# One line of scheduling: hand-written instruction order or the Tile scheduler's, in a fused linear-attention and SoLU kernel

## The chip, the cores and the metric

The kernel runs on one core of one Trainium2 chip. The metric is the device time of one execution in microseconds. Before the change the median of 3 runs is 242.95 us (242.89 to 244.39).

## The reference, cut to what matters

```
kv  = einsum('bhsd,bhse->bhde', k, v)           # per batch and head, 64 x 64
o   = einsum('bhsd,bhde->bhse', q, kv)
x   = o / sqrt(mean(o*o, -1) + 1e-6) * g_norm   # norm over the 64 columns of a head
x   = x.transpose(0,2,1,3).reshape(4608, 512)   # 8 batches x 576 tokens, 8 heads x 64
h   = x @ w_in                                  # 512 -> 1024
sm  = exp(h - max) / (sum(exp(h - max)) + 1e-9)
s   = h * sm
ln  = (s - mean(s)) / sqrt(var(s) + 1e-6) * g_ln
out = ln @ w_out                                # 1024 -> 512
```

All inputs and the output are float32. q, k and v are 8 x 8 x 576 x 64.

## The kernel before

The 4608 tokens are worked in nine chunks of 512. Chunk c below 8 holds the first 512 tokens of batch c; chunk 8 holds the last 64 tokens of all eight batches, which the code calls the remainders (`krem`, `vrem`, `qrem`). Tokens lie along the free dimension, features along the partitions.

One chunk passes these steps. `kv_mm` (L143) multiplies keys and values of a batch, and `kv_evac` (L164) copies the result into a block-diagonal tile `kvbd`. `qT` (L172) transposes the queries on TensorE in two halves and VectorE copies each half out. `o_mm` (L191) multiplies the two, one of four head pairs at a time, and ScalarE squares the result (`osq`). `s_mm` (L206) averages the squares over a head by a matmul; ScalarE takes logarithm and exponential (`lss`, `rst`), and VectorE scales into `x_sb`. `h_step` (L220) makes one of eight 128-feature blocks of h with four matmuls; ScalarE takes the exponential `e_sb`, VectorE multiplies to `u_sb`, and GpSimd (POOL) squares it (`usq_sb`, L236) and adds two exponentials (`es_sb`, L238). `stats` (L242) sums squares, values and exponentials over the features with 20 matmuls that each fill one of four 32-column strips of the array; `stats_t` (L257) turns the sums over and makes the per-token factor `rstd`. `out_half` (L279) is the second large product, eight matmuls for 128 tokens in two halves; `out_evac` (L289) scales by `rstd` and stores. The centring of `w_out` (`w_out_mean` L303, `w_out_center` L308) is done once.

There are 51 loads, all issued by POOL, whose instruction stream also holds the squares and sums: eight each of `qs`, `ks` and `vs` (L74, 512 tokens of a batch), eight each of `qrem`, `krem` and `vrem` (L82), two for `w_in` (L97) and one for `w_out` (L138). `ks`, `vs` and `qs` have three buffers each; the remainders have tiles of their own, with no buffer to wait for. The output is stored from SyncE. In PSUM, the tag `st` has one buffer, shared by `kv_ps`, `qT_ps`, `sum_ps` and `st_ps`; h has two, the output two, and `o_ps` with `s_ps` three.

The order is written out by hand. `at(c, s, fn, ...)` (L317) enters a step into a plan under chunk c and slot s; the loop at L384 calls `h_step(c, s)` and then what the plan holds for that slot. So each chunk's h steps are interleaved with the second product of the chunk before and with keys, transposes and norms of the chunks after it. The first 13 loads are written before the loop; the loads of batches 2 to 7 stand in the plan (L354 to L361). The line `tc.manual_schedule()` (L48) makes each engine keep its instructions in the order in which this code issues them.

Where that line is missing, the Tile scheduler orders every engine's instructions when the program is built. It walks along an estimated timeline and gives each engine that is free the earliest-written instruction whose inputs and buffers are ready in that estimate. The order that comes out is fixed in the program. Waits on data and buffers stay, so each engine still works its list from the front.

Of the kernel before, what the change touches and what calls it, by code (L numbers as in the profile page):

```python
# [18 lines left out]
def kernel(  # L19
# [25 lines left out]
    NC = B + 1  # L45
    REM = S - 512

    ctx.enter_context(tc.manual_schedule())  # L48
    big = ctx.enter_context(tc.tile_pool(name="big", bufs=1))
    kvl = ctx.enter_context(tc.tile_pool(name="kvl", bufs=3))  # L50
    ql = ctx.enter_context(tc.tile_pool(name="ql", bufs=3))
# [368 lines left out]
```

## Time and profile before

| | us |
|---|---|
| median of 3 runs | 242.95 |
| the profiled execution | 243.18 |
| its span, first to last instruction | 241.3 |
| TensorE (PE) busy | 199.5 (83%) |
| POOL busy | 159.4 (66%) |
| VectorE (DVE) busy | 138.0 (57%) |
| ScalarE (ACT) busy | 121.5 (50%) |

Busy times of different engines overlap. Matmuls are pipelined, so their busy times overlap among themselves too; four matmuls of 512 columns that run back to back end 0.86 us apart from the next four. 1.88 us of the profiled execution lie outside its span.

### The profile page before, as it was taken

To read this page: it belongs to the slowest core of one execution; us is meant where nothing else is said; L and a number is where in the kernel's file an instruction comes from. 1 tells how busy PE (TensorE), PEld (TensorE's weight loads), DVE (VectorE), ACT (ScalarE), POOL (GpSimd) and SP (SyncE) were. 2 spreads that over 40 slices of the span, in tenths; PEclk is the share of its full clock that TensorE was granted. 3 is DMA by queue.
4 is the path that set the end of the run, shared out by engine and by line. 5 is a ranking of instruction groups with operands and counts; after the bars stand their busy time and mean duration, and the time that the engine had idled before them with its cause. 6 is when DMAs were issued, how large, how long until landed. Compare 5 with 4: busy or idle time off the path is not lost.

```text
span 241.3 us, 3920 instructions
## 1 busy us (share of the span) xinstructions
PE 199.5 (83%) x1536; PEld 95.1 (39%) x1536; DVE 138.0 (57%) x254; ACT 121.5 (50%) x199; POOL 159.4 (66%) x165
## 2 busy tenths in 40 slices
PE   0164899557989997998999899899979989979971
PEld 0141244223444453444445444444535444444420
DVE  0723462593458756674775667487466755755431
ACT  2019453740377646666476666657667577343000
POOL 8640299574766697879959987375756738758500
PEclk9998599965999999999999999999999999999979
DMA  6999969599995289629945992021111202202233
GB/s 66 175 198 196 292 190 182 77 173 144 148 104 110 87 100 175 121 87 151 190 96 93 174 171 90 1 87 46 45 43 46 87 0 90 87 0 87 90 87 88
DMA packets 45682, 27.00 MB, mean 112 GB/s; under 512 B 14944, under 2 KB 40544, under 8 KB 45664
## 3 DMA queue, kind: packets, MB, share of 16 engines
q0 software_dynamic: 39216, 17.30, 55.9%
q1 hardware_dynamic: 6448, 9.44, 11.9%
q8 instruction: 12, 0.20, 0.4%
q14 instruction: 6, 0.05, 0.1%
HBM read 32.51 MB, written 9.44 MB: 174 GB/s over the span
## 4 chain that ended last, share of the span: by engine, by line
PE 53%; ACT 19%; DVE 16%; issue 6%; POOL 4%; POOLq 0%; ACTq 0%
PE out_ps L284 18%; PE h_ps L227 18%; ACT rst L212 5%; ACT lss L210 5%; ACT e_sb L234 5%; PE sum_ps L249 4%; DVE x_sb L213 4%; PE qT_ps L182 4%; PE mean_ps L306 3%; DVE kvbd L168 2%; ACT osq L204 2%; DVE u_sb L235 2%; PE s_ps L208 2%; PE o_ps L197 2%; DVE ob L292 1%
## 5 line engine op out<-in xcount | busy, mean ns | idle before, releaser
L236 POOL TENSOR_TENSOR usq_sb<-u_sb 128x512 bf16<-128x512 bf16 x72 | 75.0, 1043 | 62.4 <-DVE u_sb L235 62.1
L234 ACT ACTIVATE e_sb<-h_ps,zero_t 128x512 f32<-128x512 f32 x72 | 49.1, 682 | 69.8 <-PE h_ps L227 67.4
L227 PE MATMUL h_ps<-x_sb,w_in_sb 128*128 128x512 bf16 x288 | 78.1, 393 | 4.7 <-DVE x_sb L213 4.7
L284 PE MATMUL out_ps<-w_out_sb,u_sb 128*128 128x512 bf16 x288 | 75.9, 391 | 3.7 <-DVE ob L292 3.7
L235 DVE TENSOR_TENSOR u_sb<-h_ps,e_sb 128x512 bf16<-128x512 f32 x72 | 49.4, 686 | 46.4 <-ACT e_sb L234 46.3
L238 POOL TENSOR_TENSOR es_sb<-e_sb 128x512 bf16<-128x512 f32 x36 | 45.7, 1270 | 0.0
L227 PEld LDWEIGHTS <-w_in_sb 128*128 128x128 bf16 x288 | 27.9, 102 | 42.8 <-issue 15.4
L284 PEld LDWEIGHTS <-u_sb 128*128 128x128 bf16 x288 | 27.1, 100 | 38.9 <-issue 11.9
L213 DVE SCALAR_TENSOR_TENSOR x_sb<-o_ps,g_rep,rst 128x512 bf16<-128x512 f32 x36 | 27.0, 751 | 24.9 <-ACT rst L212 24.9
L204 ACT ACTIVATE osq<-o_ps,zero_t 128x512 bf16<-128x512 f32 x36 | 24.1, 678 | 15.6 <-PE o_ps L197 15.5
L292 DVE TENSOR_SCALAR ob<-out_ps,rstd 128x512 f32<-128x512 f32 x36 | 26.7, 743 | 4.8 <-PE out_ps L284 4.0
L212 ACT ACTIVATE rst<-lss,zero_t 128x512 f32<-128x512 f32 x36 | 26.0, 722 | 1.2
L210 ACT ACTIVATE lss<-s_ps,eps_t 128x512 f32<-128x512 f32 x36 | 24.5, 681 | 0.5 <-PE s_ps L208 0.5
L182 PE MATMUL qT_ps<-ident,qs 128*64 128x128 bf16 x256 | 11.5, 238 | 15.5 <-POOL ident masks.py:199 7.6
L208 PE MATMUL s_ps<-osq,head_mean 128*128 128x512 bf16 x36 | 13.7, 392 | 10.7 <-ACT osq L204 9.7
L182 PEld LDWEIGHTS <-qs 128*64 128x64 bf16 x256 | 9.1, 120 | 21.4 <-issue 13.9
L187 DVE COPY qT_sb<-qT_ps 128x1024 bf16<-128x1024 bf16 x18 | 12.3, 681 | 2.4 <-PE qT_ps L182 2.4
L197 PE MATMUL o_ps<-qT_sb,kvbd 128*128 128x512 bf16 x32 | 12.5, 411 | 1.0 <-DVE kvbd L168 1.0
L273 ACT ACTIVATE lv<-vare,zero_t 128x4 f32<-128x4 f32 x9 | 2.7, 297 | 20.6 <-DVE vare L269 20.6
L254 DVE COPY sums<-sum_ps 128x512 f32<-128x512 f32 x9 | 6.2, 691 | 8.4 <-PE sum_ps L249 8.4
L261 PEld LDWEIGHTS st_ps<-stat_pick,sums 128*128 128x128 f32 x72 | 9.3, 191 | 2.2 <-DVE qT_sb L187 0.9
L150 PEld LDWEIGHTS <-ks 128*64 128x64 bf16 x256 | 5.5, 123 | 9.7 <-issue 7.6
(49 smaller groups left out, 131.5 us busy)
## 6 DMA issues: line engine op xcount, KB each, us to landing
out_dram<-ob SPq DMA_DIRECT2D x32, 256.0 KB, 2.4
qs<-in_q_dram POOLq DMA_DIRECT2D x8, 512.0 KB, 6.4
ks<-in_k_dram POOLq DMA_DIRECT2D x8, 512.0 KB, 6.1
vs<-in_v_dram POOLq DMA_DIRECT2D x8, 512.0 KB, 8.5
w_out_f<-in_moe_w_out_dram POOLq DMA_DIRECT2D x1, 2048.0 KB, 19.4
w_in_sb<-in_moe_w_in_dram POOLq DMA_DIRECT2D x2, 512.0 KB, 12.3
out_dram<-ob SPq DMA_DIRECT2D x8, 128.0 KB, 2.3
krem<-in_k_dram POOLq DMA_DIRECT2D x8, 64.0 KB, 5.4
```

Of the source, the lines that this page charges most:

```text
L182: nc.tensor.transpose(t[hh * 64:hh * 64 + 64, pp, cols], qs[c][:, 2 * p + hh, j, :], ident[:, :])
L204: nc.scalar.activation(out=osq[:, :], in_=t[:, :], func=AF.Square, bias=zero_t[:, :])
L210: nc.scalar.activation(out=lss[:, :], in_=t[:, :], func=AF.Ln, bias=eps_t[:, :])
L212: nc.scalar.activation(out=rst[:, :], in_=lss[:, :], func=AF.Exp, scale=-0.5, bias=zero_t[:, :])
L213: nc.vector.scalar_tensor_tensor(out=x_sb[c][:, p, :], in0=o_ps.pop((c, p))[:, :], scalar=g_rep[:, :], in1=rst[:, :], op0=MUL, op1=MUL)
L227: nc.tensor.matmul(t[:, :], w_in_sb[:, dt, f * 128:(f + 1) * 128], x_sb[c][:, dt, :], start=(dt == 0), stop=(dt == NP - 1),)
L234: nc.scalar.activation(out=e[:, f % 2, :], in_=t[:, :], func=AF.Exp, bias=zero_t[:, :])
L235: nc.vector.tensor_tensor(out=u_sb[c][:, f, :], in0=t[:, :], in1=e[:, f % 2, :], op=MUL)
L236: nc.gpsimd.tensor_tensor(out=usq_sb[c][:, f, :], in0=u_sb[c][:, f, :], in1=u_sb[c][:, f, :], op=MUL)
L238: nc.gpsimd.tensor_tensor(out=es_sb[c][:, f // 2, :], in0=e[:, 0, :], in1=e[:, 1, :], op=ADD)
L284: nc.tensor.matmul(t[:, :], u_sb[c][:, f, m * 128:(m + 1) * 128], w_out_sb[:, f, :], start=(f == 0), stop=(f == NF - 1),)
L292: nc.vector.tensor_scalar_mul(out=ob[:, :], in0=t[:, :], scalar1=rstd_sb[c][:, m:m + 1])
```

## The change

The line that asks for the hand-written order is taken out. Nothing else is edited: the same instructions are issued by the same code, in the same written order, with the same tiles and buffers.

```diff
     NC = B + 1
     REM = S - 512
 
-    ctx.enter_context(tc.manual_schedule())
     big = ctx.enter_context(tc.tile_pool(name="big", bufs=1))
     kvl = ctx.enter_context(tc.tile_pool(name="kvl", bufs=3))
```

## Rows read from the trace of the kernel before

**Rows 1.** The page, busy time: us, share of the span, instructions.

```profile
PE 199.5 (83%) x1536; PEld 95.1 (39%) x1536; DVE 138.0 (57%) x254; ACT 121.5 (50%) x199; POOL 159.4 (66%) x165
```

**Rows 2.** Windows: us, busy of PE, PEld, DVE, ACT, POOL, granted clock, DMA share, GB/s.

```profile
40.00:60.00 20.00, 13.26 (x88) 5.85 (x87) 10.76 (x17) 7.11 (x11) 12.63 (x14) 0.75 1.17 135
100.00:120.00 20.00, 18.99 (x158) 9.23 (x155) 14.05 (x25) 12.65 (x22) 17.26 (x19) 1.00 0.86 124
```

**Rows 3.** Timeline of the start: start us, us, engine, line, instruction, [idle before <- releaser].

```profile
7.58 1.13 DVE L123 CAST stat_pick<-ident 32x3 f32<-32x3 bf16 x4 [5.92 <-POOL ident masks.py:199]
...
13.77 0.68 POOL L82 DMA_DIRECT2D vrem<-in_v_dram  x1 [1.77 <-DMA vs<-in_v_dram]
14.22 1.07 PE L150 MATMUL kv_ps<-vs,ks 128*64 128x64 bf16 x32 [0.78 <-DVE qT_sb L187]
...
15.31 0.91 POOL L138 DMA_DIRECT2D w_out_f<-in_moe_w_out_dram  x1
...
27.94 1.04 POOL L236 TENSOR_TENSOR usq_sb<-u_sb 128x512 bf16<-128x512 bf16 x1 [11.71 <-DVE u_sb L235]
```

**Rows 4.** DMA issues at 3.19, 7.49, 8.39 and 13.77 us: size, us to landing.

```profile
vs<-in_v_dram POOLq DMA_DIRECT2D x1, 512.0 KB, 10.3
...
ks<-in_k_dram POOLq DMA_DIRECT2D x1, 512.0 KB, 14.6
...
vs<-in_v_dram POOLq DMA_DIRECT2D x1, 512.0 KB, 16.4
...
vrem<-in_v_dram POOLq DMA_DIRECT2D x1, 64.0 KB, 11.9
```

**Rows 5.** The page, DMA issues: the load of `w_out`.

```profile
w_out_f<-in_moe_w_out_dram POOLq DMA_DIRECT2D x1, 2048.0 KB, 19.4
```

**Rows 6.** The page, costliest groups: busy us, mean ns | idle before, releaser.

```profile
L236 POOL TENSOR_TENSOR usq_sb<-u_sb 128x512 bf16<-128x512 bf16 x72 | 75.0, 1043 | 62.4 <-DVE u_sb L235 62.1
...
L238 POOL TENSOR_TENSOR es_sb<-e_sb 128x512 bf16<-128x512 f32 x36 | 45.7, 1270 | 0.0
```

**Rows 7.** Load issues by line: ns min/median/max on POOL, first and last start us.

```profile
L74 POOL DMA_DIRECT2D ks<-in_k_dram x8: 892/942/943, 2.3 to 128.5; - x8
...
L82 POOL DMA_DIRECT2D qrem<-in_q_dram x8: 722/726/729, 71.8 to 139.9; - x8
```

**Rows 8.** Timeline of PE, 42 to 64 us.

```profile
46.49 0.38 PE L208 MATMUL s_ps<-osq,head_mean 128*128 128x512 bf16 x1 [1.39 <-ACT osq L204]
...
48.98 0.38 PE L208 MATMUL s_ps<-osq,head_mean 128*128 128x512 bf16 x1 [1.89 <-ACT osq L204]
...
50.59 0.59 PE L227 MATMUL h_ps<-x_sb,w_in_sb 128*128 128x512 bf16 x1 [0.81 <-DVE x_sb L213]
...
55.76 1.06 PE L182 MATMUL qT_ps<-ident,qs 128*64 128x128 bf16 x16 [2.16 <-DVE kvbd L168]
56.75 1.89 PE L284 MATMUL out_ps<-w_out_sb,u_sb 128*128 128x512 bf16 x4
58.43 1.91 PE L227 MATMUL h_ps<-x_sb,w_in_sb 128*128 128x512 bf16 x4
...
61.24 0.62 PE L249 MATMUL sum_ps<-usq_sb,stat_sel 128*32 128x512 bf16 x8
...
62.44 1.04 PE L227 MATMUL h_ps<-x_sb,w_in_sb 128*128 128x512 bf16 x4
```

**Rows 9.** The chain of waits, one chunk: start us, us, what.

```profile
106.00 0.86 PE out_ps L284 x4
106.86 1.19 PE sum_ps L249 x20
...
128.07 1.19 PE sum_ps L249 x20
```

**Rows 10.** Timeline, the one longer PE wait inside that chunk.

```profile
114.47 0.38 PE L208 MATMUL s_ps<-osq,head_mean 128*128 128x512 bf16 x1 [0.75 <-ACT osq L204]
```

## The prediction

> **What bounds the kernel now.** I read the busy shares first, then stretches of 20 us, then the chain of waits, then the timelines of the stretches that stood out. PE is the busiest engine with 199.5 us of 241.3, POOL the second with 159.4 [rows 1]. From about 85 us on PE is full: 18.99 us of 20 at a granted clock of 1.00 [rows 2]. There one chunk takes 128.07 - 106.86 = 21.2 us, and the chain runs from one PE group to the next at 0.86 us per four matmuls [rows 9]; the only longer wait that PE has inside that chunk is 0.75 us for a square [rows 10]. So a new order can win little there and can only lose by giving PE something that isn't ready. What is loose is the front. Up to 28 us the kernel waits for its first loads and for one chain of dependent steps. Between 40 and 60 us PE is busy for 13.26 us and its granted clock averages 0.75 of full speed [rows 2]: it waits 1.39, 1.89, 0.81 and 2.16 us for ScalarE and VectorE steps of chunk 1 [rows 8], 6.25 us in all. A greedy order attacks just these waits, and it also moves POOL's loads.
>
> **The start, -0.7 us.** VectorE's casts at 7.58 us waited 5.92 us for the identity matrix [rows 3], and everything written behind them stood still, the clearing of `kvbd` included, which needs no input. A scheduler that takes what is ready does that clearing first, and the copies of the transposed queries come earlier. The product of keys and values started at 14.22 us after 0.78 us of waiting for such a copy [rows 3]. Its own input, the first `vs`, was issued at 3.19 us and landed 10.3 us later [rows 4], at 13.49. So the gain stops there: 14.22 - 13.49 = 0.7 us. Bounds 0 and -0.7; I take all of it.
>
> **POOL's loads and the first squares, +5.1 us.** This is the step that I think decides. POOL issues 51 loads from the same stream as the squares. In the hand order 13 are issued by 16.2 us (the last at 15.31 for 0.91) and the first square follows at 27.94, after 11.71 us in which POOL had nothing to do [rows 3]. The scheduler will not leave that hole. 23 loads need no buffer to come free: `ks`, `vs` and `qs` of batch 2 (third buffers), the 12 `krem` and `vrem` of batches 2 to 7, and the 8 `qrem`. They are ready from the start and go ahead of the first square. On POOL they take 3 x 0.94 + 20 x 0.73 = 17.4 us [rows 7]. But an issue also waits: the eleventh load stood 1.77 us, up to 13.77 us, for the third to land [rows 3], 0.3 us after that landing. So a load waits for the one eight before it. The landings go in order: the second `ks` at 7.49 + 14.6 = 22.1 us, its `vs` at 8.39 + 16.4 = 24.8, the second `vrem` at 13.77 + 11.9 = 25.7 [rows 4], `w_out` at 15.31 + 19.4 = 34.7 [rows 3, 5]. That is 2.7 us for a load of 512 KB and 0.45 us for each of the two remainders after it. After 34.7 the 23 take 3 x 2.7 + 20 x 0.45 = 17.1 us, up to 51.8. The last of the 23, number 36, waits for number 28, which lands 8 x 0.45 earlier at 48.2. With its own 0.73 us the first square starts at 48.9 instead of 27.94.
>
> Who waits: the sums of chunk 0 need its 8 squares and 4 additions, 8 x 1.043 + 4 x 1.270 = 13.4 us of POOL [rows 6]. They would be done at 62.3. The hand order reached these sums at 61.24 us [rows 8], so this alone costs 62.3 - 61.2 = 1.1 us. If `ks`, `vs` and `qs` of batch 3 go ahead too (their buffers are free once batch 0 has been used, near 15 us), 3 x 2.7 = 8.1 us more pass: 70.4, and the cost is 9.2 us. Whether they go ahead hangs on when the estimate has the first square ready, which no row shows. The bounds are +1.1 and +9.2 (and 0, if POOL's order stays as it was); nothing is nearer to either, so I take the middle, 5.1. PE's queue is what stands behind: the sums share the one `st` buffer with the transposes of chunk 2, and behind them stand chunk 1's h steps and chunk 0's output.
>
> By the Trainium skill's page "DMA: Bandwidth & Descriptors", section "Anatomy of one DMA — SWDGE (gpsimd) path", a load takes some 2.0 us plus its bytes over 436 GB/s, an estimate of 6.8 us for `w_out`; loads would then land early and this term would be near zero. The trace has 19.4 us for that load [rows 5], behind others in the queue, and the measurement decides.
>
> **The clock, +1.7 us.** After the waits of 46 to 56 us the next groups of four took 1.89 and 1.91 us, where 62.44 has 1.04 [rows 8]: half speed, the lower of PE's two levels (1.2 against 2.4 GHz), 0.85 + 0.87 = 1.7 us. A PE that waits for POOL at the sums pays the like once more. Bounds 0 and 1.7; the wait is longer than those in the rows, so I take 1.7.
>
> **The gaps at 46 to 56 us, 0.** The scheduler can pull transposes, `o_mm` and `s_mm` of chunk 1 into PE's idle time before 40 us. Worth up to 6.25 us [rows 8], but whatever PE wins before the sums of chunk 0 it then waits for POOL. That cover is the delay above; without it the 6.25 us are won. Bounds 0 and -6.25.
>
> **Steady chunks and the end, 0.** From the second chunk on PE has a backlog, and the earliest written of what is ready is the hand order again. Bounds per chunk: -0.75, the wait above [rows 10], and +3.1 (a rival below). SyncE's stores keep their order. The end is a chain through POOL's last squares in either order.
>
> **The sum.** -0.7 + 5.1 + 1.7 = +6.1 us on the profiled execution's 241.3 us span, 247.4; with the 1.88 us outside the span 249.3. That execution took 243.18, 0.23 above the median, so against the median 242.95 + 6.1 = 249.0.
>
> **Rivals.** *The gaps close and POOL is not late: faster.* If the scheduler's estimate has POOL as busy with loads as the chip shows, the first square stays near 28 us and chunk 1 is ready when chunk 0 ends: -0.7 - 6.25 = -7, 236.0 us. For it speaks that these waits are long and that the work to fill them exists; against it that the filling matmuls hang on loads that land at 25 us and later [rows 4], and a PE that has them in front stands still. The point that decides is the number of loads ahead of the first square. With 33, the last waits for number 25 at 46.9 us, the squares are done near 61 and nothing is lost; with 25, it waits for number 17 at 41.0, they are done at 55.1 and all of the 6.25 us is won.
>
> *Nothing measurable: about 242.4 us.* The written order is already the order of readiness, only the -0.7 us remains.
>
> *The strips are pulled apart: much slower.* The 20 sums take 1.19 us because four strips run at a time; one by one, at 0.86 / 4 = 0.215 us each, they would take 4.3, so 3.1 us more per chunk [rows 9]. A scheduler that places each sum when its square is done scatters them between other matmuls. If half of the gain is lost, 1.55 x 9 = 14 us: 257. The Trainium skill's page "TensorE: Matmul & The Clock Gate", Part 3, states that matmuls on different column groups run concurrently when issued together; 20 in 1.19 us agrees. Against this rival: with a backlog on PE the squares are all there when the sums' turn comes.
>
> **The numbers.** Forecast case 0.38 (by itself 244 to 253 us), faster rival 0.30 (230 to 240), no change 0.17, strips 0.15 (250 to 270). The predicted time is the forecast's, 249.0 us. The range of 8 in 10 leaves out the lower third of the faster rival and some two thirds of the strips' case: 234 to 259. About 1% (2.4 us) is what runs of this kernel tell from no change: faster 0.30, within it 0.17, slower 0.53.
>
> **What would show it.** POOL's first square near 49 to 57 us with more than 33 loads before it; a PE wait for POOL at the first sums; a clock below full behind it. Wrong, if the first square stays near 28 us, if PE has no wait for POOL, or if the steady chunk moves from 21.2 us by more than 0.8: then the change lives where I put zero.

## The result, and the profile after

The changed kernel is **faster**: 233.93 us (median of 4 runs, 233.62 to 235.9) against 242.99 (median of 4, 242.89 to 244.39) of the kernel before on the same chip, a ratio of 0.9636 with a 95% interval of 0.9581 to 0.9691. The prediction was 249.0 us, range 234 to 259, so it missed the sign. The profiled execution took 233.9 us with a span of 231.9, 9.4 us less than the span of before.

Line numbers after are one less than before. The page's busy times:

```profile
PE 197.1 (85%) x1510; PEld 95.6 (41%) x1536; DVE 142.3 (61%) x254; ACT 120.9 (52%) x199; POOL 159.6 (69%) x165
```

Two windows, with the columns of [rows 2]:

```profile
40.00:60.00 20.00, 18.36 (x115) 8.07 (x117) 15.10 (x24) 12.25 (x20) 19.32 (x20) 1.00 0.94 111
100.00:120.00 20.00, 19.77 (x170) 9.70 (x172) 14.37 (x26) 13.07 (x22) 15.78 (x15) 1.00 0.72 129
```

PE has the same work in a shorter span. Between 40 and 60 us it is busy 18.36 us, not 13.26, and in the full part 19.77, not 18.99 [rows 2]. The chain of waits gives the steady chunk:

```profile
106.22 1.19 PE sum_ps L248 x20
126.42 1.19 PE sum_ps L248 x20
146.62 1.19 PE sum_ps L248 x20
```

126.42 - 106.22 = 20.2 us, where [rows 9] had 21.2. The 20 sums still take 1.19 us, so in the steady chunks nothing pulled the strips apart.

The place of the 9.4 us is read from the start of each chunk's sums on PE. Chunk 0's start at 61.15 us, before at 61.24 [rows 8]: the whole front gave 0.1 us. From there to chunk 3's it is 65.19 us instead of 66.76, so 1.6 less. From chunk 3 to chunk 8 it is 91.2 instead of 97.18, 6.0 less. From chunk 8's sums to the end it is 14.36 instead of 16.1, 1.8 less (rounded, 9.4 in all). Most of the gain lives in the full part of the kernel, where the prediction had put zero.

The front did change a great deal. The timeline of PE after, first 95 us:

```profile
25.11 0.29 PE L149 MATMUL kv_ps<-vs,ks 128*64 128x64 bf16 x3 [7.03 <-DMA vs<-in_v_dram]
...
31.81 1.03 PE L226 MATMUL h_ps<-x_sb,w_in_sb 128*128 128x512 bf16 x2
...
34.68 3.75 PE L305 MATMUL mean_ps<-w_out_f,g_mean 128*128 128x512 f32 x4 [0.56 <-DMA w_out_f<-in_moe_w_out_dram]
...
69.20 0.38 PE L196 MATMUL o_ps<-qT_sb,kvbd 128*128 128x512 bf16 x1 [1.53 <-DVE x_sb L212]
...
70.61 1.91 PE L226 MATMUL h_ps<-x_sb,w_in_sb 128*128 128x512 bf16 x4 [0.33 <-issue]
...
92.94 0.38 PE L207 MATMUL s_ps<-osq,head_mean 128*128 128x512 bf16 x1 [1.12 <-ACT osq L203]
```

The scheduler put keys and values of batch 1 ahead of chunk 0's averaging, and PE stood 7.03 us for a load. So the first h block came at 31.81 us, and POOL's first square with it:

```profile
25.93 0.89 POOL L73 DMA_DIRECT2D qs<-in_q_dram  x1
40.61 2.04 POOL L235 TENSOR_TENSOR usq_sb<-u_sb 128x512 bf16<-128x512 bf16 x2 [13.79 <-DVE u_sb L234]
```

POOL did not wait for loads there, but 13.79 us for values. 18 loads stood ahead of that square, not the 36 of the prediction.

What changed in a steady chunk is seen on ScalarE and VectorE. Two stretches of the kernel before, VectorE and then ScalarE:

```profile
111.18 0.75 DVE L213 SCALAR_TENSOR_TENSOR x_sb<-o_ps,g_rep,rst 128x512 bf16<-128x512 f32 x1 [0.64 <-ACT rst L212]
...
112.44 0.16 DVE L269 SCALAR_TENSOR_TENSOR vare<-sq,var 128x4 f32<-128x4 f32 x1
...
112.64 0.30 ACT L273 ACTIVATE lv<-vare,zero_t 128x4 f32<-128x4 f32 x1 [1.49 <-DVE vare L269]
112.97 0.30 ACT L275 ACTIVATE rstd<-lv,zero_t 128x4 f32<-128x4 f32 x1
113.17 0.67 ACT L234 ACTIVATE e_sb<-h_ps,zero_t 128x512 f32<-128x512 f32 x1
113.74 0.68 ACT L204 ACTIVATE osq<-o_ps,zero_t 128x512 bf16<-128x512 f32 x1
```

The square `osq` for which PE waits 0.75 us [rows 10] is late because a logarithm of 4 columns, `lv`, stands in front of it and waits 1.49 us for `vare`, which stands on VectorE behind an `x_sb`. The same place after:

```profile
131.46 0.16 DVE L268 SCALAR_TENSOR_TENSOR vare<-sq,var 128x4 f32<-128x4 f32 x1
131.54 0.74 DVE L212 SCALAR_TENSOR_TENSOR x_sb<-o_ps,g_rep,rst 128x512 bf16<-128x512 f32 x1
...
131.66 0.30 ACT L272 ACTIVATE lv<-vare,zero_t 128x4 f32<-128x4 f32 x1 [0.96 <-DVE vare L268]
131.86 0.67 ACT L233 ACTIVATE e_sb<-h_ps,zero_t 128x512 f32<-128x512 f32 x1
132.43 0.28 ACT L274 ACTIVATE rstd<-lv,zero_t 128x4 f32<-128x4 f32 x1
132.62 0.67 ACT L203 ACTIVATE osq<-o_ps,zero_t 128x512 bf16<-128x512 f32 x1
```

The statistics stand ahead of `x_sb`, the logarithm waits 0.96 us, and the exponential goes between the two small steps. PE shows no wait of 0.1 us or more in that chunk.

### The profile page after: what moved, and what is told of

Its sections match the earlier page's. It is cut to its first block, busy times and chain, and to the rows that moved or that the text cites. A ratio compares the mean times of both kernels' runs of the same rounds, so it can differ in the third digit from the quotient of the medians.

```text
span 231.9 us, 3917 instructions
## 1 busy us (share of the span) xinstructions
PE 197.1 (85%) x1510; PEld 95.6 (41%) x1536; DVE 142.3 (61%) x254; ACT 120.9 (52%) x199; POOL 159.6 (69%) x165
## 4 chain that ended last, share of the span: by engine, by line
PE 58%; POOL 15%; DMA 13%; DVE 6%; ACT 4%; issue 3%; POOLq 0%
PE out_ps L283 21%; PE h_ps L226 18%; DMA w_out_f<-in_moe_w_out_dram 8%; POOL usq_sb L235 5%; DMA vs<-in_v_dram 4%; PE sum_ps L248 4%; PE mean_ps L305 4%; PE st_ps L260 3%; POOL es_sb L237 3%; PE s_ps L207 3%; PE qT_ps L181 2%; DVE sq L264 2%; POOL ks L73 2%; POOL qs L73 2%; ACT osq L203 2%
## 5 line engine op out<-in xcount | busy, mean ns | idle before, releaser
L226 PE MATMUL h_ps<-x_sb,w_in_sb 128*128 128x512 bf16 x279 | 76.0, 387 | 1.9 <-DVE x_sb L212 0.8
L283 PE MATMUL out_ps<-w_out_sb,u_sb 128*128 128x512 bf16 x274 | 72.5, 379 | 2.7 <-DVE ob L291 1.4
L283 PEld LDWEIGHTS <-u_sb 128*128 128x128 bf16 x288 | 26.4, 98 | 32.6 <-issue 3.7
L291 DVE TENSOR_SCALAR ob<-out_ps,rstd 128x512 f32<-128x512 f32 x36 | 26.1, 743 | 3.0 <-PE out_ps L283 2.3
L181 PE MATMUL qT_ps<-ident,qs 128*64 128x128 bf16 x256 | 12.5, 246 | 10.9 <-POOL ident masks.py:199 8.4
L167 DVE CAST kvbd<-kv_ps 64x256 bf16<-64x256 f32 x16 | 6.7, 419 | 14.9 <-PE kv_ps L158 14.7
L207 PE MATMUL s_ps<-osq,head_mean 128*128 128x512 bf16 x36 | 14.4, 405 | 1.7 <-ACT osq L203 1.3
L149 PE MATMUL kv_ps<-vs,ks 128*64 128x64 bf16 x256 | 7.3, 210 | 8.7 <-DMA vs<-in_v_dram 8.6
L196 PE MATMUL o_ps<-qT_sb,kvbd 128*128 128x512 bf16 x29 | 11.3, 405 | 2.9 <-DVE x_sb L212 1.5
```

Source lines behind the costliest of these rows:

```text
L181: nc.tensor.transpose(t[hh * 64:hh * 64 + 64, pp, cols], qs[c][:, 2 * p + hh, j, :], ident[:, :])
L226: nc.tensor.matmul(t[:, :], w_in_sb[:, dt, f * 128:(f + 1) * 128], x_sb[c][:, dt, :], start=(dt == 0), stop=(dt == NP - 1),)
L283: nc.tensor.matmul(t[:, :], u_sb[c][:, f, m * 128:(m + 1) * 128], w_out_sb[:, f, :], start=(f == 0), stop=(f == NF - 1),)
L291: nc.vector.tensor_scalar_mul(out=ob[:, :], in0=t[:, :], scalar1=rstd_sb[c][:, m:m + 1])
```

## The experiments

Theory A was that the gain comes from this order on ScalarE and VectorE, theory B that it comes from PE's own order. The table gives the median of 4 runs, the ratio to the kernel before on the same chip with its 95% interval, the start of chunk 0's sums, the time from there to chunk 3's, and the steady chunk (chunks 3 to 5).

| kernel | us | ratio | first sums | to chunk 3 | steady |
|---|---|---|---|---|---|
| before | 242.99 | | 61.24 | 66.76 | 21.2 |
| changed | 233.93 | 0.9636 (0.9581 to 0.9691) | 61.15 | 65.19 | 20.2 |
| e1 PE by hand | 234.02 | 0.9625 (0.9583 to 0.9667) | 58.78 | 66.27 | 20.2 |
| e2 only PE free | 237.52 | 0.9765 (0.9735 to 0.9796) | 66.87 | 61.63 | 20.2 |
| e3 batch 1 later | 232.99 | 0.9599 (0.9548 to 0.9649) | 62.11 | 65.40 | 20.2 |
| e4 hand, rstd late | 235.06 | 0.9656 (0.962 to 0.9693) | 61.81 | 64.60 | 20.7 |
| e5 hand, two moves | 232.43 | 0.9578 (0.9524 to 0.9633) | 61.32 | 62.99 | 20.0 |
| e6 only ACT free | 236.21 | 0.9737 (0.9678 to 0.9796) | 61.57 | 65.85 | 20.7 |
| e7 only DVE free | 231.47 | 0.9537 (0.9479 to 0.9595) | 60.45 | 63.78 | 20.35 |
| e8 only POOL free | 248.23 | 1.0232 (1.0172 to 1.0291) | 62.07 | 72.47 | 21.2 |
| e9 hand, front rewritten | 227.83 | 0.9354 (0.9319 to 0.9388) | 56.91 | 63.00 | 20.0 |
| e10 e9, DVE free | 225.41 | 0.9257 (0.9202 to 0.9313) | 53.76 | 62.68 | 20.0 |
| e11 POOL by hand | 229.81 | 0.9448 (0.9399 to 0.9496) | 59.00 | 61.06 | 20.2 |
| e12 statistics from PSUM | 233.25 | 0.9639 (0.953 to 0.9748) | 59.79 | 65.74 | 20.2 |

**e1 and e2: PE against the rest.**

```diff
-    ctx.enter_context(tc.manual_schedule())
+    ctx.enter_context(tc.manual_schedule(engines={mybir.EngineType.PE}))     # e1
+    ctx.enter_context(tc.manual_schedule(engines={mybir.EngineType.Activation,
+        mybir.EngineType.DVE, mybir.EngineType.Pool, mybir.EngineType.SP}))  # e2
```

> Only TensorE keeps the hand-written order; ScalarE, VectorE, POOL and SyncE are ordered by the scheduler. Theory A (the gain of 9 us comes from the order on ScalarE and VectorE: the small statistics steps no longer stand between an exponential and the square that TensorE waits for): the steady chunk is 20.2 to 20.6 us, not 21.2; the 7 us wait of TensorE for the values of batch 1 is absent because their product is back in its hand place; total 230 to 236 us. Theory B (the gain comes from TensorE's own order, which fills its waits with whatever is ready): steady chunk 21.0 to 21.3, total 240 to 243 us.

> The reverse half: only TensorE is ordered by the scheduler; ScalarE, VectorE, POOL and SyncE keep the hand-written order. Theory A (gain from ScalarE and VectorE): steady chunk 21.0 to 21.3 us and the waits of 0.75 to 1 us for squares are still there; the front is no better than before, total 241 to 247 us. Theory B (gain from TensorE's own order): steady chunk 20.2 to 20.4 us, total 233 to 236 us.

e1 came out as A says, and e2's steady chunk as B says: 20.2 us in both. So neither theory holds as an either-or: each half of the order alone takes the wait away. In e2 the logarithm still waits 1.49 us on ScalarE, but PE has the matmuls of keys and values in front of the one that needs the square, where the hand order has them behind it:

```profile
114.15 0.30 ACT L273 ACTIVATE lv<-vare,zero_t 128x4 f32<-128x4 f32 x1 [1.49 <-DVE vare L269]
...
115.17 0.69 PE L150 MATMUL kv_ps<-vs,ks 128*64 128x64 bf16 x32
...
116.00 0.39 PE L208 MATMUL s_ps<-osq,head_mean 128*128 128x512 bf16 x1
```

e2 loses in the front what it wins later: PE stands 6.21 us for the values of batch 1 and 4.21 for `w_out`, and the first sums start at 66.87 us, in e1 at 58.78. Its steady chunks keep the 20 sums together, but late in the kernel it did scatter sums: three of chunk 7's squares are summed at 195.07 us and the others from 206.22.

**e3: the 7 us wait.**

```diff
+    def kv_mm_behind(b):
+        with tc.issue_after(mark["s", 0, NP - 1]):   # chunk 0's last s_mm
+            kv_mm(b)
-    at(0, 2, kv_mm, 1)
+    at(0, 2, kv_mm_behind, 1)
```

> The changed kernel with one edit: the matmuls of keys and values of batch 1 must come behind chunk 0's last averaging matmul on TensorE. Theory A1 (TensorE, standing 7 us in front of the values of batch 1, loses that time for good): first h group at 22 to 26 us instead of 31.81, chunk 0's sums 3 to 6 us earlier, total 228 to 231 us. Rival A2 (the front is bound by w_out, which lands at 34.6 us, and what TensorE loses before that it gets back from work pulled ahead): sums of chunk 0 within 1 us of 61.15, total 233 to 235 us.

This did not take the wait away. It held the keys and values behind one averaging matmul of chunk 0, the last written, and that one ran as the third of the four. PE then stood 5.10 us for the values of batch 1, with the fourth still behind them:

```profile
25.02 0.53 PE L149 MATMUL kv_ps<-vs,ks 128*64 128x64 bf16 x12 [5.10 <-DMA vs<-in_v_dram]
25.49 0.61 PE L207 MATMUL s_ps<-osq,head_mean 128*128 128x512 bf16 x1
```

So theory A1 was not put to its test. The first h block came at 28.41 us, not at 22 to 26, PE then stood 3.39 us for `w_out` at 34.66, and the first sums stayed at 62.11. That fits the rival's number, and does not show its reason. The profiled execution is also the longest of its four, 235.15 us against 232.83 to 233.05. The 0.9 us against the changed kernel are less than the two intervals tell apart.

**e4 and e5: the steady gain by hand.**

```diff
+    def stats_r(c):              # e4: lv and rstd, taken out of stats_t
+        at(c + 1, 3, stats_r, c)   # ... one slot later, ahead of out_evac(c, 0)
-            at(a - 2, 4, kv_mm, a)
-            at(a - 2, 4, kv_evac, a)
+            plan.setdefault((a - 2, 4), [])[:0] = [(kv_mm, (a,)), (kv_evac, (a,))]   # e5
```

> The kernel before, all by hand, with one edit: the two small ScalarE steps that make the factor per token (logarithm and exponential) are issued one slot later, behind the exponential of the next h block, just ahead of the output step that reads them. Theory A (the steady gain is this logarithm, which waits 1.49 us at the head of ScalarE's queue in front of an exponential and a square): the wait of 0.75 us for a square shrinks to 0.2 or less, steady chunk 20.3 to 20.6 us, total 236 to 239 us. If VectorE's order (the scaling of x ahead of the statistics) matters as much: steady chunk 20.7 to 21.0, total 239 to 241 us. Theory B (TensorE's own order gives the gain): steady chunk 21.1 to 21.3, total 242 to 243.5 us.

> All by hand, e4 and one more move: keys and values of batch c+2, with the copy into kvbd, are written at the head of slot 4, ahead of the fifth slot's averaging matmul and its x_sb, not behind them. Theory: e4's steady chunk of 20.72 us still holds one wait, 0.68 us of TensorE for the copy into kvbd, which stands on VectorE behind an x_sb; without it the chunk is 20.2 us as in the scheduled kernels, and five to six such chunks give 231.5 to 233 us. Rival: the copy is late for ScalarE's or TensorE's reasons and the wait moves to the averaging matmul, chunk 20.6 to 20.8, total 234.5 to 235.5.

In e4 the wait for the square is gone, with only `lv` and `rstd` moved. The chunk of 20.72 us is the second case of the expectation, where VectorE's order matters as much: the next wait shows, on the copy into `kvbd`:

```profile
116.43 0.64 PE L182 MATMUL qT_ps<-ident,qs 128*64 128x128 bf16 x16 [0.68 <-DVE kvbd L168]
```

That is the 0.26 us wait of the kernel before at this place, grown to 0.68: of the 0.75 + 0.26 us, 0.49 are won (21.21 to 20.72). e5 moves the matmuls of keys and values ahead of an averaging matmul on PE, and so the copy ahead of an `x_sb` on VectorE, and takes the rest: 19.97 us, less than the scheduler's 20.2. So two moves by hand give the whole steady gain. The first, on ScalarE alone, is shown by itself; in the second PE's order changes together with VectorE's, as in e2, and what each of the two gives is not told apart. e4's total is below its expectation, since the chunks after the fifth gain more and the end is 1.7 us shorter (below).

**e6, e7, e8: one engine at a time.** In each, one engine is left out of the set in `manual_schedule(engines={...})`.

> Only ScalarE is ordered by the scheduler, the other four engines by hand. The scheduler puts an exponential and a square ahead of the small logarithm in the steady chunk. Theory (a stalled head of one queue, which any engine's new order can take away): like e4, steady chunk 20.6 to 20.8 us, total 234 to 237. Rival (the engines' orders must fit one another, a single free one doesn't help): 21.0 to 21.3, total 241 to 244.

> Only VectorE is ordered by the scheduler, the other four by hand. In the first chunks its list has the four statistics steps behind x_sb as by hand. Theory (a stalled head of one queue): later on the statistics stand ahead of x_sb, the logarithm at the head of ScalarE's queue no longer waits 1.49 us, steady chunk 20.2 to 20.7 us, total 232 to 237. Rival (ScalarE's place for the logarithm decides alone): steady chunk 21.0 to 21.3, total 241 to 244.

> Only POOL is ordered by the scheduler, the other four by hand. This is the step on which the prediction stood, by itself: 18 loads stand ahead of the first square, not the 36 of the prediction, and the 18th waits for the tenth, so the first square stays at 28 to 29 us. Expected: sums of chunk 0 at 61 to 62 us, steady chunk 21.2, total 242 to 244. If POOL's order by itself were worth something, for better or worse, the total would lie outside 241 to 245.5, with a TensorE wait for POOL or later loads to show for it.

ScalarE alone does what e4 did. VectorE alone is worth 11.4 us, more than all five engines together. It puts the statistics ahead of `x_sb`, and keeps 0.56 us of the start too (first keys and values at 13.66 us, before at 14.22). POOL alone costs 5.3 us, against the expectation:

```profile
35.17 0.69 POOL L82 DMA_DIRECT2D krem<-in_k_dram  x1 [5.09 <-DMA w_out_f<-in_moe_w_out_dram]
37.43 0.68 POOL L82 DMA_DIRECT2D vrem<-in_v_dram  x1 [1.58 <-DMA ks<-in_k_dram]
38.13 2.04 POOL L236 TENSOR_TENSOR usq_sb<-u_sb 128x512 bf16<-128x512 bf16 x2
...
65.97 1.07 POOL L236 TENSOR_TENSOR usq_sb<-u_sb 128x512 bf16<-128x512 bf16 x1
...
67.09 0.59 PE L249 MATMUL sum_ps<-usq_sb,stat_sel 128*32 128x512 bf16 x1 [4.40 <-POOL usq_sb L236]
```

The first four rows are POOL's, the last PE's. 22 loads stand ahead of the first square, which starts at 38.13 us instead of 27.94; 39 loads are out by the eighth square at 65.97, where the hand order has 20 at 49.97. PE waits 4.40 us at chunk 0's sums.

**e9 and e10: what the front is worth.**

```diff
+    load_kv(2); load_rem(krem, k, 2); load_rem(vrem, v, 2); load_q(2)   # behind w_out's load
-    at(0, 5, w_out_mean)
+    plan[0, 5] += [(w_out_mean, (0, 3))]
+    plan[0, 6] += [(w_out_mean, (3, 6))]
+    plan[0, 7][-1:-1] = [(w_out_mean, (6, 8))]
-    at(1, 0, kv_mm, 2)
-    at(1, 0, kv_evac, 2)
+    at(0, 7, kv_mm, 2)
+    at(0, 7, kv_evac, 2)
```

The centring is split too: four blocks stay in slot 7 of chunk 0 and four go to slot 0 of chunk 1. The loads of batch 3 take the place that batch 2's had, and e5's two moves are in it.

> All by hand, e5 and the front rewritten: the four loads of batch 2 stand ahead of the first square (as in the scheduled kernel, 18 loads instead of 13 and then one more by the same count), the loads of batch 3 take their old place, the 16 matmuls of the mean of w_out are split in three parts between chunk 1's averaging matmuls, and keys and values of batch 2 come ahead of chunk 1's first h block. Theory: the waits of 1.39, 1.89, 0.81 and 2.16 us between 46 and 56 us come from the order, not from data, and close; sums of chunk 0 at 55 to 58 us instead of 61.32, steady chunk still 20.0 us, total 226 to 229.5. Rival: the loads of batch 2 or the squares on POOL are the true limit and the waits move to them, sums of chunk 0 at 60 to 62, total 231 to 233.5.

> e9 with VectorE alone ordered by the scheduler. If VectorE's order in e9 costs time in the front (copies behind the identity casts, scalings behind centrings), 0.5 to 1.5 us less than e9; if not, the same within 0.5 us in the front and a steady chunk of 20.0 to 20.35 us, so up to 2 us more.

The long waits of [rows 8] were the order's: with these moves the longest left there is 0.70 us, and the first sums start at 56.91 us. Which of them did it (the mean of `w_out` split among chunk 1's norms, the earlier loads, the earlier keys and values) is not told apart. VectorE's free order gives 3.2 us more in the front, twice the most that was expected, and e5's steady chunk stays. e10, at 225.41 us, beats both kernels; it is 17 to 18 us under the kernel before.

**e11 and e12: what POOL's order costs in the changed kernel.** e11 has `engines={mybir.EngineType.Pool}`, the rest by the scheduler. e12 is the changed kernel with:

```diff
-        nc.vector.tensor_tensor(out=sq[:, :, :], in0=st[:, :, 1:3], in1=st[:, :, 1:3], op=MUL)
-        var = work.tile([128, 4], FP32, name="var")
-        nc.vector.tensor_tensor(out=var[:, :], in0=st[:, :, 0], in1=sq[:, :, 0], op=SUB)
+        nc.vector.tensor_tensor(out=sq[:, :, :], in0=st_ps[:, :, 1:3], in1=st[:, :, 1:3], op=MUL)
+        nc.vector.tensor_tensor(out=st_ps[:, :, 0], in0=st_ps[:, :, 0], in1=sq[:, :, 0], op=SUB)
...
-            out=vare[:, :], in0=sq[:, :, 1], scalar=1e-6 * d_ff * d_ff, in1=var[:, :], op0=MUL, op1=ADD
+            out=vare[:, :], in0=sq[:, :, 1], scalar=1e-6 * d_ff * d_ff, in1=st_ps[:, :, 0], op0=MUL, op1=ADD
```

> The reverse of e8: only POOL keeps the hand-written order, the other four engines are ordered by the scheduler. e8 showed that POOL's new order alone costs 5.3 us. Theory C (that cost is covered in the changed kernel, since TensorE's own late start of h, at 31.81 us, leaves POOL idle until 40.6 us anyway, and the early loads of batch 2 are then worth something): POOL by hand gains nothing, sums of chunk 0 at 61 to 67 us, total 233 to 238. Rival (the cost is there in the changed kernel too): sums of chunk 0 at 56 to 59 us, total 228 to 231.

> The changed kernel, all by the scheduler, with one edit: the small VectorE steps of the statistics (squares, variance and its correction) each take one operand from PSUM where they took both from SBUF; the number of steps is the same. In the changed kernel these steps of 0.16 us stood up to 1.57 us and ended 0.02 to 0.03 us after the POOL square beside them, while the steps with a PSUM operand (u_sb, x_sb) never did. Theory D (what POOL's new order costs in the changed kernel comes to TensorE by this road: packed POOL work holds the statistics, these hold the logarithm at the head of ScalarE's queue, that holds the square): the steps take 0.2 us or less each, the logarithm's wait of 2.01 us at 91 us and TensorE's of 1.53 and 1.12 us behind it go, sums of chunk 2 at 102 to 104 us instead of 106.15, total 229.5 to 232. Rival (POOL's lateness itself, its loads and squares, is what costs): the steps get short but the sums of chunk 2 stay at 105.5 to 106.5, total 233 to 234.5.

Theory C fell: POOL by hand, with the other four free, takes 229.81 us, some 4.1 less than the changed kernel. Theory D fell as well. Its first half is right: the statistics' steps are 0.15 to 0.17 us and the waits of 1.53 and 1.12 us are gone, so chunk 1's sums start at 79.86 us, as early as in e11 (79.66). But there PE meets POOL itself:

```profile
83.73 0.51 PE L248 MATMUL sum_ps<-usq_sb,stat_sel 128*32 128x512 bf16 x1 [3.25 <-POOL usq_sb L235]
...
85.45 1.89 PE L226 MATMUL h_ps<-x_sb,w_in_sb 128*128 128x512 bf16 x4
```

It waits 3.25 us for a square, runs at half pace behind it, and reaches chunk 2's sums at 105.33, where the changed kernel has 106.15 and e11 99.86. So POOL's own lateness is the limit there, and VectorE's stalls took the same time ahead of it. One doubt stays on the stage times of e11: its profiled execution (span 225.7 us) is the shortest of its four runs, 227.55 to 230.55, and the price of 4.1 us is that of the medians.

## Why the prediction was wrong, point by point

- **The start, -0.7.** Right in size where it can be seen by itself: e7 has the first keys and values at 13.66 us, 0.56 earlier, and the first sums 0.8 us earlier. In the changed kernel they start at 13.68 too, but PE then stands 7.03 us in front of the values of batch 1, and at the first sums 0.1 us is left.
- **POOL's loads, +5.1.** The cost is real, 5.3 us by itself (e8) and 4.1 among the other engines (e11), so sign and size were right. By chunk 8's sums e8 is 6.5 us late (231.71 against 225.18), and its shorter end gives 1.7 back. The working held in part. In e8 the 21st load waits 5.09 us for `w_out`, the 13th, so "the one eight before it" holds; and with 22 loads ahead that working gives 34.7 + 2.7 + 0.7 = 38.1 us for the first square, where 38.13 was measured. The count was wrong: 22 loads, not 36, stand ahead of it (18 in the changed kernel), and the rest of the delay comes from the 17 loads set between the squares. In the changed kernel chunk 0's h was late already and nothing waits for POOL at its sums; in e12 POOL's cost falls on chunk 1's.
- **The clock, +1.7.** Such stretches are there: groups at half pace from 31.81 to 38 us (shown below), and one of 1.91 us at 70.61 behind a wait of 1.53. The kernel before has its own [rows 8], and the windows' granted clock, which rose from 0.83 and 0.75 to 1.00 between 20 and 60 us, misses the first of these. So the step's sign is not shown.
- **The gaps at 46 to 56 us, 0.** In the changed kernel they close, but PE stands 7.03 us at 25 us and reaches the first sums no earlier, so 0 is what came out, though not under the cover named (POOL). That the 7 us are what took the gain is not shown, since e3 left 5.10 of them. e9 and e10, which have no such wait, show what can be won: 4.4 and 6.7 us by the first sums against e5's 61.32 and e7's 60.45.
- **Steady chunks, 0. This is the step that failed.** It said that with a backlog on PE "the earliest written of what is ready is the hand order again". That is true of PE in the changed kernel, whose steady chunk has the hand order, and false of ScalarE and VectorE, whose hand order held instructions that were not ready (in e2, where those two kept it, it is false of PE). The wait of 0.75 us [rows 10] was in the text as a bound for one chunk, and went into no sum and no rival; what the square itself was waiting for was not followed, and the 0.26 us behind it was left out. They made 1.0 us per chunk and 7.6 us from chunk 0's sums to chunk 8's (163.94 to 156.39), with POOL's cost already paid out of it.
- **The end, 0.** It gave 1.8 us, and the order is not shown as the cause. Before, the last 16 matmuls took 5.30 us at a granted clock of 0.69 of full speed (232 to 236 us), so partly at the lower level; in e8, behind the same waits of 1.44 and 1.42 us, they took 3.61. Kernel before, then e8:

```profile
231.02 5.30 PE L284 MATMUL out_ps<-w_out_sb,u_sb 128*128 128x512 bf16 x16 [1.42 <-DVE ob L292]
```

```profile
237.53 3.61 PE L284 MATMUL out_ps<-w_out_sb,u_sb 128*128 128x512 bf16 x16 [1.42 <-DVE ob L292]
```

What lets the clock fall in the one and not in the other stays open; all other profiles here have 3.61 too. Three executions of the kernel before on two other chips took 240.55 to 240.67 us, some 2.3 under its median; whether theirs was the shorter end no trace shows. So 1.7 us of the gain, and of every figure here against the kernel before, may not be the order's.

The faster rival's 236.0 us lies near the result, but its two terms are not what happened: the front's gaps gave nothing in the end, and POOL was late.

## What to carry to other kernels

A wait that recurs in every chunk is to be followed one step further than the engine that shows it: here PE's 0.75 us for a square was a 4-column logarithm at the head of ScalarE's queue, and two moves by hand (e5) gave 1.5 us more than the scheduler on all engines. Each engine's order is a change of its own: VectorE's was worth -11.4 us, ScalarE's -6.7, PE's -5.6 and POOL's +5.3, and they don't add, as the first three remove the same wait. In this kernel the queue that mixes loads with compute was better left in hand order, and the engine to give to the scheduler was the one where short steps of several chains meet; on another kernel both are to be tried.

## What the runs showed of the hardware

Short VectorE steps that read only SBUF stood still while POOL worked. VectorE and POOL of the changed kernel:

```profile
66.92 1.57 DVE L266 TENSOR_TENSOR var<-st,sq 128x4 f32<-128x4 f32 x1
...
67.40 1.06 POOL L235 TENSOR_TENSOR usq_sb<-u_sb 128x512 bf16<-128x512 bf16 x1
...
130.17 1.04 POOL L235 TENSOR_TENSOR usq_sb<-u_sb 128x512 bf16<-128x512 bf16 x1 [1.73 <-DVE u_sb L234]
...
130.48 0.17 DVE L262 COPY st<-st_ps 128x12 f32<-128x12 f32 x1 [0.39 <-PE st_ps L260]
130.69 0.54 DVE L264 TENSOR_TENSOR sq<-st 128x8 f32<-128x8 f32 x1
```

`var` and `sq` ended 0.02 to 0.03 us after the POOL square (68.49 after 68.46, 131.23 after 131.21); alone they take 0.16 to 0.17. The copy `st`, which reads PSUM, took 0.17 us beside the same square. With one of two operands in PSUM (e12) such a step took 0.17 us while a square ran:

```profile
109.15 1.04 POOL L235 TENSOR_TENSOR usq_sb<-u_sb 128x512 bf16<-128x512 bf16 x1 [1.33 <-DVE u_sb L234]
...
109.67 0.17 DVE L264 TENSOR_TENSOR sq<-st_ps,st 128x8 f32<-128x8 f32 x1
```

The Trainium skill's page "Trainium Architecture — The Big Picture", section "What this means for kernel authors", says that VectorE and GpSimd share a pair of SBUF ports, and that it is an exclusive lock and not a split of bandwidth. The trace agrees for the squares. Stalls beside load issues are there too, but not at each and not up to their end: a `var` at 90.06 took 0.96 us, inside two issues from 89.94 to 91.33, and an `sq` at 66.72 took 0.17 beside one.

The granted clock did not tell PE's pace in the front. The window from 20 to 40 us reads 1.00 in the changed kernel and in e11, yet in the changed kernel two h matmuls took 1.03 us at 31.81 and four of the mean 3.75 at 34.68; e11 has two such groups, at 31.01 and 34.77, in little over half the time:

```profile
31.01 0.59 PE L227 MATMUL h_ps<-x_sb,w_in_sb 128*128 128x512 bf16 x2
...
34.77 1.98 PE L306 MATMUL mean_ps<-w_out_f,g_mean 128*128 128x512 f32 x4 [0.39 <-DMA w_out_f<-in_moe_w_out_dram]
```

Both PEs had waited about 7 us up to 25 us (7.03 and 7.11), so the wait alone does not tell the two apart either; what does stays open. The pace of known groups has to be read beside the clock.
